# Two chunks of a linear-attention kernel: k and r turned by DMA transposes and not by TensorE

## The chip, the cores and the metric

The kernel runs on one core of a Trainium2 chip. The metric is device time in microseconds, the median of the runs; a profiled execution gives the span from its first to its last instruction and, beside it, that execution's own time.

## The reference, cut to what matters

A recurrent linear attention over 4 batches, 8 heads, 768 steps and 48 columns a head feeds a token and channel mixer. The inputs r, k, v are f32, the result is f32.

```
for t in range(S):
    cur = einsum('bhd,bhe->bhde', u[None] * kt, vt)
    y[:, :, t] = einsum('bhd,bhde->bhe', rt, state + cur)
    state = w[None, :, :, None] * state + einsum('bhd,bhe->bhde', kt, vt)
x = y.transpose(0, 2, 1, 3).reshape(B, S, H * D)
h = maximum(xt @ w_tok1, 0) @ w_tok2          # xt: x with steps and columns exchanged
u = x + h.transpose(0, 2, 1)
out = u + maximum(u @ w_ch1, 0) @ w_ch2
```

## The kernel before, in words

Each batch is cut into six chunks of 128 steps. A chunk's work: k, r and v are loaded (`kt`, `rt`, `vt`); k and r are multiplied by powers of the decay w into one bf16 tile `kr`; that tile is turned so that the head's columns lie on partitions (`rk`); TensorE multiplies the turned k and r to scores of step against step (`at_ps`); VectorE masks them (`AT`); TensorE multiplies `AT` and v, and the turned r and the carried state `S`, to `y_ps`; and the products of k and v are added to the state in `kv_ps`. The step's own term with u is formed beside it: `ku`, `rku`, a sum `adg`, and `yd`. The sum of `y_ps` and `yd` goes to `x_b`.

Then the mixer of the batch: `h_ps` and `h1r` (token mixing), `hx_ps` or `hT_ps` (back), a turned sum `uT`, `z_ps` and `zr` (up), `h_ps` and `osb` (down; these carry the name of the token tile in the profile), and a store. The mixer of one batch is interleaved with the chunks of the next: while TensorE does the second batch's mixer, GpSimd and the queues prepare the third batch's chunks, here called 0 to 5.

The third and the fourth batch take their chunks in pairs, (0, 1), (2, 3), (4, 5): one task writes the scores of both chunks of a pair. In these batches all products with k and r are made by GpSimd (POOL), in order.

How a chunk's `kr` is turned is told by the table `STYLES`, one entry a chunk. `pe` means eight transposes on TensorE into a PSUM bank `tr_ps`, followed by one copy to `rk` by VectorE or ScalarE. `dma` means one DMA transpose from `kr` to `rk`, issued by SyncE (SP). Before the change chunks 0 and 1 of the third batch are `pe`, and chunks 2 to 5 and the whole fourth batch are `dma`:

```
if STYLE[n][0] == "dma":
    L["rk"] = sb("rk", [128, 2, HP, T], bf16)
    sp.dma_start_transpose(L["rk"].rearrange("p j a s -> p (j a) s"),
                           L["kr"].rearrange("p j h d -> p (j h d)"))
else:
    for j in range(2):
        for a in range(HP):
            pe.transpose(L["tr"][:, j, a, :], pair(L["kr"][:, j], a), ident)
    copy(on, L["rk"], L["tr"])
```

All work is recorded as tasks first and then emitted in the order of the table `ORDER`, written out by hand; every engine runs its own instructions in that order, and waits by semaphores for the others. SP issues in one queue, in order, all loads of k, r and v, the DMA transposes of `kr` and of the mixer's `u_sb`, and the stores. `BUFS` gives each new tile its buffer: `m` are the seven PSUM banks that scores, `y_ps`, `z_ps`, `h_ps`, `hx_ps` and `tr_ps` share. `ENGINES` says who takes a task that two engines could do. Nearly all instructions carry line L287 of the profile, that of a helper, so they are told apart by tile names.

Of the kernel before, what the change touches and what calls it, by code (L numbers as in the profile page):

```python
# [11 lines left out]
f32 = mybir.dt.float32  # L12
# [6 lines left out]
Ln = ACTF.Ln  # L19

ORDER = [
# [41 lines left out]
]  # L63
BUFS = {
    'AT0': [
# [41 lines left out]
],  # L107
    'osb': [
    0, 1, 2, 2, 1, 0, 2, 1, 2, 0, 1, 2, 0, 2, 0, 1, 0, 1, 2, 1, 0, 2, 1, 0, 2,
# [32 lines left out]
    0, 1, 2, 1, 0, 2,  # L142
],
    'yd': [
    0, 1, 2, 0, 1, 2, 0, 1, 2, 1, 2, 0, 1, 2, 0, 1, 2, 0,
],
    'ydb': [
    0, 1, 0, 1, 0, 1,
# [15 lines left out]
]  # L164
W_DEP = [(0, 2, 2), (0, 5, 0), (0, 5, 0), (0, 3, 2), (1, 2, 0), (1, 1, 2), (1, 3, 0)]
HOLD = {(0, 4, 1): (0, 2, 1),
# [28 lines left out]
 [(0, 1), (2, 3), (4, 5)]]  # L195
STYLES = [
  ('f32', 'pe'), ('f32', 'pe'), ('f32', 'pe'), ('f32', 'pe'), ('f32', 'pe'), ('f32', 'pe'), ('f32', 'pe'),
  ('f32', 'pe'), ('f32', 'pe'), ('f32', 'pe'), ('f32', 'pe'), ('f32', 'pe'), ('pe', 'dve'), ('pe', 'dve'),
  ('dma', 'dve'), ('dma', 'dve'), ('dma', 'dve'), ('dma', 'dve'), ('dma', 'dve'), ('dma', 'dve'),
  ('dma', 'dve'), ('dma', 'dve'), ('dma', 'dve'), ('dma', 'dve'),  # L200
]
# [1038 lines left out]
```

## Time and profile before

| | |
|---|---|
| median of 3 runs | 163.56 us (163.2 to 163.7) |
| the profiled execution's own time | 162.75 us |
| its span | 161.0 us |
| TensorE busy, share of the span | 153.0 us, 95% |
| VectorE busy | 113.5 us, 70% |
| GpSimd busy | 89.3 us, 55% |
| ScalarE busy | 67.7 us, 42% |
| granted TensorE clock, mean | 0.997 |
| SP's and ACT's DMA queue, share of 16 engines | 70.3% |

The page cuts the span in 40 slices of 4.0 us. DMA landing is the time from the start of an issue to the last of its semaphore updates. SP has no busy time of its own: an issue is listed with its start and its duration, in which waits and a full queue are contained. A merged row, such as x2, reaches from the first start to the last end.

### The profile page before, as it was taken

The numbers are of one execution on the slowest core, as the hardware profiler recorded it, in microseconds if no ns is written. First come the engines' busy times: TensorE is split into PE (matmuls) and PEld (weight loads), VectorE is DVE, ScalarE is ACT, GpSimd is POOL, SyncE is SP. The second block draws the span as 40 slices with busy tenths as digits, with TensorE's granted clock in tenths as the row PEclk, the third lists the DMA queues.
The fourth block names the chain that finished last, engine by engine and source line by source line (L and its number), as shares of the span: only waits on it lengthen the run. The fifth ranks groups of instructions, "written<-read, shape, count | busy, mean of one in ns | idle before, by whom it ended". The sixth has DMA issues, their size and how long they took to land.

```text
span 161.0 us, 3815 instructions
## 1 busy us (share of the span) xinstructions
PE 153.0 (95%) x1475; PEld 102.1 (63%) x1475; DVE 113.5 (70%) x244; ACT 67.7 (42%) x150; POOL 89.3 (55%) x113
## 2 busy tenths in 40 slices
PE   6888789999999999999999999999999999999992
PEld 1354567776666777676776755766667666666661
DVE  6699695767574898789889876788988263852142
ACT  3977985567924243435144241047820202252000
POOL 7049892004788897999999998969422000000000
PEclk9999999999999999999999999999999999999998
DMA  4998899999999999999999997999620157200052
GB/s 124 202 213 165 149 206 211 210 209 196 224 210 211 173 232 178 252 236 171 186 193 224 196 184 150 240 201 197 137 77 4 49 122 219 98 4 0 0 195 98
DMA packets 90948, 26.35 MB, mean 164 GB/s; under 512 B 85682, under 2 KB 90036, under 8 KB 90932
## 3 DMA queue, kind: packets, MB, share of 16 engines
q1 hardware_dynamic: 88576, 22.88, 70.3%
q0 software_dynamic: 2160, 3.15, 11.7%
q8 instruction: 11, 0.18, 0.5%
q10 hardware_dynamic: 196, 0.11, 0.2%
q14 instruction: 5, 0.04, 0.1%
HBM read 20.46 MB, written 4.72 MB: 156 GB/s over the span
## 4 chain that ended last, share of the span: by engine, by line
PE 71%; DMA 10%; issue 9%; POOL 4%; ACT 2%; DVE 1%; SPq 1%; POOLq 0%
PE h_ps L287 34%; PE z_ps L287 23%; DMA vt<-in_v_dram 5%; DMA kt<-in_k_dram 5%; PE y_ps L287 4%; PE hT_ps L287 3%; PE at_ps L287 3%; PE kv_ps L287 2%; POOL wch L287 1%; POOL kr L287 1%; PE hx_ps L287 1%; PE tr_ps L287 1%; POOL pr L287 1%; PE trk L287 1%; ACT vb L287 1%
## 5 line engine op out<-in xcount | busy, mean ns | idle before, releaser
L287 PE MATMUL h_ps<-wch,zr 128*128 128x384 bf16 (+1 forms) x300 | 53.9, 320 | 0.0
L287 PE MATMUL z_ps<-uT,wch 128*128 128x384 bf16 x288 | 51.8, 326 | 0.0
L287 ACT ACTIVATE zr<-z_ps 128x384 bf16<-128x384 f32 x56 | 26.2, 492 | 41.8 <-PE z_ps L287 39.5
L287 PEld LDWEIGHTS <-wch 128*128 128x128 bf16 x288 | 31.4, 114 | 12.5
L287 PEld LDWEIGHTS <-zr 128*128 128x128 bf16 x300 | 27.4, 98 | 15.4 <-issue 0.2
L287 DVE TENSOR_TENSOR AT<-at_ps,mask 128x512 bf16<-128x512 f32 x48 | 30.6, 684 | 3.5 <-PE at_ps L287 2.9
L287 DVE TENSOR_SCALAR zr<-z_ps 128x384 bf16<-128x384 f32 x40 | 21.3, 553 | 12.5 <-PE z_ps L287 12.5
L287 POOL TENSOR_TENSOR kr<-kt,wnat 128x384 bf16<-128x384 f32 x20 | 19.9, 1005 | 2.8 <-DMA kt<-in_k_dram 2.7
L287 POOL TENSOR_TENSOR yd<-vb,adg 128x384 f32<-128x384 bf16 x17 | 13.9, 829 | 8.6 <-DVE x_b L287 4.2
L287 PEld LDWEIGHTS <-kr 128*128 128x128 bf16 x192 | 12.1, 97 | 6.8 <-DVE kr L287 1.8
L287 DVE TENSOR_TENSOR osb<-u_sb,h_ps 128x384 f32<-128x384 bf16 (+1 forms) x16 | 8.2, 526 | 9.7 <-PE h_ps L287 9.5
L287 ACT CAST vb<-vt 128x384 bf16<-128x384 f32 x22 | 11.0, 512 | 5.9 <-DMA vt<-in_v_dram 5.8
L287 POOL TENSOR_TENSOR rku<-ku,rt 128x384 f32<-128x384 f32 x12 | 12.0, 1000 | 0.2
L287 POOL TENSOR_TENSOR ku<-kt,u_bc 128x384 f32<-128x384 f32 x12 | 12.0, 1001 | 0.0
L287 POOL TENSOR_TENSOR kr<-rt,wp 128x384 bf16<-128x384 f32 x12 | 11.9, 1001 | 0.0
L287 DVE TENSOR_TENSOR x_b<-y_ps,yd 128x384 bf16<-128x384 f32 x18 | 9.5, 553 | 3.1 <-PE y_ps L287 1.4
L287 DVE TENSOR_TENSOR u_sb<-x_b,hT_ps 128x384 bf16<-128x384 bf16 x15 | 7.7, 551 | 4.5 <-PE hT_ps L287 4.4
L287 POOL DMA_DIRECT2D wch<-in_moe_w_ch_dram x5 | 3.4, 674 | 13.1 <-DMA kt<-in_k_dram 13.1
L287 PEld LDWEIGHTS <-wtok 128*128 128x128 bf16 x78 | 7.4, 98 | 4.5
L287 PE MATMUL h_ps<-x_b,wtok 128*128 128x384 bf16 x48 | 8.8, 326 | 0.0
L287 PE MATMUL y_ps<-vb,AT 128*128 128x48 bf16 x192 | 8.7, 183 | 0.0
L287 PEld LDWEIGHTS <-AT 128*128 128x128 bf16 x192 | 7.1, 96 | 0.3 <-DVE AT L287 0.2
(96 smaller groups left out, 180.4 us busy)
## 6 DMA issues: line engine op xcount, KB each, us to landing
kt<-in_k_dram SPq DMA_DIRECT2D x24, 192.0 KB, 4.2
vt<-in_v_dram SPq DMA_DIRECT2D x24, 192.0 KB, 4.0
out_dram<-osb SPq DMA_DIRECT2D x23, 192.0 KB, 2.2
win<-in_r_dram SPq DMA_DIRECT2D x6, 384.0 KB, 5.5
rt<-in_r_dram SPq DMA_DIRECT2D x12, 192.0 KB, 4.4
wch<-in_moe_w_ch_dram POOLq DMA_DIRECT2D x4, 384.0 KB, 6.1
wtok<-in_moe_w_tok_dram POOLq DMA_DIRECT2D x2, 384.0 KB, 6.8
wch<-in_moe_w_ch_dram POOLq DMA_DIRECT2D x1, 768.0 KB, 9.1
```

The source lines that it names most:

```text
L287: return lambda *args, **kw: tc.keep_in_program_order(f(*args, **kw))
```

## The change

The entries of chunks 0 and 1 of the third batch become `dma`. Two tasks fall away (the copies from PSUM), so later tasks get lower numbers, and the order and the buffers are written anew from there on.

```diff
 STYLES = [
...
-  ('f32', 'pe'), ('f32', 'pe'), ('f32', 'pe'), ('f32', 'pe'), ('f32', 'pe'), ('pe', 'dve'), ('pe', 'dve'),
+  ('f32', 'pe'), ('f32', 'pe'), ('f32', 'pe'), ('f32', 'pe'), ('f32', 'pe'), ('dma', 'dve'), ('dma', 'dve'),
...
 ORDER = [
...
-    306, 411, 414, 407, 412, 394, 307, 416, 532, 429, 536, 89, 330, 415, 92, 422, 533, 395, 417, 419, 431, 313, 88,
+    306, 411, 414, 407, 412, 394, 307, 416, 532, 429, 536, 330, 415, 89, 395, 417, 419, 533, 92, 422, 431, 313, 396,
...
```

The instructions of the first and the second batch, of the setup and of the fourth batch keep their order on every engine. What moves lies in the third batch's chunks and the second batch's mixer.

First, SP's queue from the middle of the second batch's last loads. `kr_72` is the tile of chunk 0, `kr_68` that of chunk 1, `kr_70` and `kr_71` those of chunks 3 and 2. Before:

```order
L287 DMA vt<-in_v_dram 128x8x48
L287 DMA rt<-in_r_dram 128x8x48
L287 DMA kt<-in_k_dram 128x8x48
L287 DMA out_dram<-osb 128x384 x2
L287 DMA rt<-in_r_dram 128x8x48 x2
L287 DMA_TRANSPOSE rk<-kr_70 128x8x128
L287 DMA_TRANSPOSE rk<-kr_71 128x8x128
L287 DMA kt<-in_k_dram 128x8x48
L287 DMA_TRANSPOSE uT<-u_sb 128x9x128
```

and now:

```order
L286 DMA_TRANSPOSE rk<-kr_72 128x8x128
L286 DMA vt<-in_v_dram 128x8x48
L286 DMA out_dram<-osb 128x384
L286 DMA rt<-in_r_dram 128x8x48
L286 DMA kt<-in_k_dram 128x8x48
L286 DMA_TRANSPOSE rk<-kr_68 128x8x128
L286 DMA rt<-in_r_dram 128x8x48 x2
L286 DMA_TRANSPOSE rk<-kr_70 128x8x128
L286 DMA_TRANSPOSE rk<-kr_71 128x8x128
L286 DMA_TRANSPOSE uT<-u_sb 128x9x128
```

Two transposes are new, one ahead of a `vt`, one ahead of the two `rt` of chunks 3 and 4; the two stores stand apart and earlier by a place or two; `uT` now stands ahead of the `kt` behind chunk 2's transpose. Six rows between the two `rt` and `kr_70` (vt, kt, out, rt, vt, kt), alike in both, are left out. All that follows, the transposes of chunks 4 and 5 with it, keeps its order.

Second, TensorE around the scores of chunks 0 and 1, matmuls alone. Before:

```order
L287 MATMUL tr_ps<-ident,kr_72 128x128
L287 MATMUL hx_ps<-ident,x_b_99 128x128
L287 MATMUL tr_ps<-ident,kr_68 128x128
L287 MATMUL hx_ps<-wtok_101,h1r 128x384
L287 MATMUL at_ps<-rk 128x128
L287 MATMUL hT_ps<-h1r,wtok_101 128x384
L287 MATMUL z_ps<-uT,wch_0_102 128x384
```

and now:

```order
L286 MATMUL hx_ps<-ident,x_b_99 128x128
L286 MATMUL hx_ps<-wtok_101,h1r 128x384
L286 MATMUL hT_ps<-h1r,wtok_101 128x384
L286 MATMUL z_ps<-uT,wch_0_102 128x384
L286 MATMUL z_ps<-uT,wch_1_103 128x384
L286 MATMUL at_ps<-rk 128x128
```

The two times eight transposes are gone, and the scores of chunks 0 and 1 now follow four `hT_ps` and nine `z_ps` matmuls (three z tiles) that stood behind them. The scores of chunks 2 and 3 move likewise, behind eight `h_ps` matmuls of the down projection and three small ones that stood behind them. Those of chunks 4 and 5 keep their place.

Third, VectorE from the last `x_b` of the second batch. Before:

```order
L287 TENSOR_TENSOR x_b_99<-y_ps,yd 128x384 x3
L287 COPY rk<-tr_ps 128x1024
L287 TENSOR_SCALAR h1r<-h_ps 128x384
L287 COPY osb<-h_ps 128x384
L287 TENSOR_REDUCE adg<-rku 128x8
L287 CAST uT<-hx_ps 128x3x128
L287 TENSOR_TENSOR AT_1445<-at_ps,mask 128x512
L287 TENSOR_TENSOR AT_1455<-at_ps,mask 128x512
L287 TENSOR_TENSOR u_sb<-x_b_99,hT_ps 128x384
```

and now:

```order
L286 TENSOR_TENSOR x_b_99<-y_ps,yd 128x384 x3
L286 TENSOR_SCALAR h1r<-h_ps 128x384
L286 COPY osb<-h_ps 128x384
L286 TENSOR_REDUCE adg<-rku 128x8
L286 CAST uT<-hx_ps 128x3x128
L286 TENSOR_TENSOR u_sb<-x_b_99,hT_ps 128x384
L286 TENSOR_SCALAR zr<-z_ps 128x384
L286 TENSOR_TENSOR AT_1443<-at_ps,mask 128x512
L286 TENSOR_TENSOR AT_1447<-at_ps,mask 128x512
```

The two copies from `tr_ps` are gone (the second stood behind `adg`), and the masks of chunk 0 stand behind one `u_sb` and one `zr`. On POOL only the product `kr_68` from `rt` moves, two places ahead; on ScalarE one store copy and one cast of v change places with their neighbours.

More of the change, by code (lines that the diff above doesn't have):

```diff
@@ L144 @@
     'yd': [
-    0, 1, 2, 0, 1, 2, 0, 1, 2, 1, 2, 0, 1, 2, 0, 1, 2, 0,
+    0, 1, 2, 0, 2, 1, 0, 1, 2, 1, 2, 0, 1, 2, 0, 1, 2, 0,
 ],
```

75 rows, old and new, of tables (BUFS, ENGINES, ORDER) are left out of this document.

## The prediction

> **What bounds the kernel now.** I read the slices of the page first, then the chain of waits, then what TensorE waits for, then SP's queue.
>
> ```profile
> span 161.0 us, 3815 instructions
> PE   6888789999999999999999999999999999999992
> DMA  4998899999999999999999997999620157200052
> ```
>
> TensorE is full from the seventh slice (24 us) to the last but one. The 16 DMA engines are full as well, up to slice 28 (113 us): two resources are at their limit at once. In the chain of waits, in order of time (start, us, what), all is TensorE from 43.98 on, but for 0.01 us of issue, until the last store:
>
> ```profile
> 43.98 0.40 PE trk L287 x4
> 63.37 0.45 PE tr_ps L287 x8
> 66.75 0.45 PE tr_ps L287 x8
> 68.51 0.55 PE at_ps L287 x16
> 69.49 0.49 PE z_ps L287 x3
> 78.65 0.55 PE at_ps L287 x16
> 87.08 0.55 PE at_ps L287 x16
> 92.19 3.90 PE h_ps L287 x24
> 157.83 0.02 issue
> ```
>
> The two `tr_ps` pieces are the transposes that go. The three `at_ps` pieces are the scores of the third batch's pairs (0, 1), (2, 3) and (4, 5). The `z_ps` piece is one tile of the up projection (0.49), and the `h_ps` piece gives 3.90 / 24 = 0.163 for a matmul of 384 columns. A microsecond taken from TensorE here, or put into its way, shows at the end. The windows 60 to 90 (engine busy with counts, then clock, DMA share, GB/s) and the one wait of TensorE after 44 us say the same:
>
> ```profile
> 60.00:70.00 10.00, 10.00 (x122) 7.09 (x121) 8.36 (x16) 3.98 (x10) 9.13 (x11) 1.00 1.03 216
> 70.00:80.00 10.00, 10.00 (x94) 7.00 (x93) 8.52 (x18) 4.03 (x9) 9.92 (x11) 1.00 0.99 193
> 80.00:90.00 10.00, 10.00 (x103) 6.86 (x100) 9.02 (x19) 3.42 (x8) 10.00 (x13) 1.00 1.20 212
> PE trk L287 <- DVE kr L287: 0.2, 1, 0.2
> ```
>
> In order: PE, weight loads, VectorE, ScalarE, POOL. TensorE is full, at a granted clock of 1.00; POOL has 0.95 us to spare in thirty; the DMA share is about 1 or more. So what is put on the DMA engines here has no idle time to go to, and all depends on how much lead the transfers have over TensorE.
>
> **What is removed.** Sixteen transposes leave TensorE: 0.45 + 0.45 = 0.90 us, on the chain. Their two copies leave VectorE, in the tile view of `rk`:
>
> ```profile
> L287 DVE COPY rk<-tr_ps x2: 679/680/682, 64.4 to 67.7; 128x1024 bf16<-128x1024 bf16 x2
> DMA to landing us min/median/max: 3.1/3.4/4.7
> ```
>
> That is 1.36 us off the chain, counted at nothing: TensorE is full through it. The second row is for the DMA transposes that the kernel has already.
>
> **What is added.** Two DMA transposes in SP's queue. Its issues (start, us, what) around the place, and later:
>
> ```profile
> 59.46 1.09 SPq L287 DMA_DIRECT2D vt<-in_v_dram  x1
> 60.60 1.72 SPq L287 DMA_DIRECT2D rt<-in_r_dram  x1
> 62.42 0.94 SPq L287 DMA_DIRECT2D kt<-in_k_dram  x1
> 63.41 1.19 SPq L287 DMA_DIRECT2D out_dram<-osb  x2
> 64.64 1.22 SPq L287 DMA_DIRECT2D rt<-in_r_dram  x2
> 69.11 1.00 SPq L287 DMA_DIRECT2D vt<-in_v_dram  x1
> 70.56 0.69 SPq L287 DMA_DIRECT2D kt<-in_k_dram  x1
> 71.36 4.01 SPq L287 DMA_TRANSPOSE rk<-kr  x2
> 75.43 0.57 SPq L287 DMA_DIRECT2D kt<-in_k_dram  x1
> 80.22 2.67 SPq L287 DMA_TRANSPOSE rk<-kr  x2
> 82.93 1.84 SPq L287 DMA_DIRECT2D rt<-in_r_dram  x2
> 91.58 3.69 SPq L287 DMA_TRANSPOSE rk<-kr  x2
> 95.32 0.57 SPq L287 DMA_DIRECT2D kt<-in_k_dram  x1
> 98.43 1.41 SPq L287 DMA_TRANSPOSE uT<-u_sb  x1
> ```
>
> Each issue begins as the one before ends; the only hole is 0.45 us, 70.11 to 70.56, until the queue waits for `u_sb` at 98.43. SP is thus always late here and waits for the transfers, not for engines. A transpose holds the queue from its start to the next start: (75.43 - 71.36) / 2 = 2.04 us, (82.93 - 80.22) / 2 = 1.36, (95.32 - 91.58) / 2 = 1.87. These are the bounds; the first pair also pays for the loads queued ahead of it, so I take the middle of the other two, 1.6 us. Two of them are 3.2; less the hole, everything behind them on SP is **2.75 us later** (2.27 to 3.63). Since SP waits for no engine there, nothing shortens this before 98 us.
>
> [...]
>
> **Who waits for what stands behind them.** Chunk 4's transpose is the second of the pair at 80.22; with a slot of 1.36 it is issued at 81.58. The transposes' landing times put it down at 85.0 (median) to 86.3 (longest). The load behind it:
>
> ```profile
> rt<-in_r_dram SPq DMA_DIRECT2D x1, 192.0 KB, 4.1
> ```
>
> is the one issued at 82.93, and lands at 87.0. A load's slot is (71.36 - 59.46) / 13 = 0.92 us, so I take 86.1 for the transpose before it. The scores that read it start at 87.08: a lead of **0.9 us** (0.7 to 2.1). After the change it lands at 86.1 + 2.75 = 88.85. TensorE would be there at 87.08 - 0.90 = 86.2, and has to wait. Behind these scores on TensorE stand down and up projections and all the rest; nothing else can run. The scores start 88.85 + 0.1 or so, and against before the end is 2.75 - 0.9 = **1.85 us later**; with the bounds, 2.27 - 2.1 = +0.2 to 3.63 - 0.7 = +2.9.
>
> The earlier pairs wait too, but these waits are parts of the same one, since SP's clock does not depend on TensorE. Chunk 1's transpose is issued after chunk 0's (59.46 + 1.6) and the slots of vt 1.14, rt 1.82, kt 0.99 and the two stores 1.23: at 66.2, landing 69.3 to 70.9. TensorE reaches its scores, moved behind four `hT_ps` (4 x 0.163 = 0.65) and three z tiles (3 x 0.49), at 68.51 - 0.90 + 2.12 = 69.7: a wait of nothing to 1.2, I take 0.3. Chunk 2's transpose is the second of the pair at 71.36 and lands about 77.3; now 80.0. Its scores, moved by eight `h_ps` matmuls (8 x 0.163 = 1.30) and three small ones (0.11), are reached at 78.65 - 0.90 + 1.41 = 79.2: a wait of 0.8.
>
> Moving these scores takes cover from the masks:
>
> ```profile
> 78.25 0.55 DVE L287 TENSOR_REDUCE adg<-rku 128x8 f32<-128x384 f32 x1
> 79.25 2.48 DVE L287 TENSOR_TENSOR AT<-at_ps,mask 128x512 bf16<-128x512 f32 x4
> 81.61 0.36 PE L287 MATMUL y_ps<-vb,AT 128*128 128x48 bf16 x8
> ```
>
> The four masks of a pair take 2.48 us, start 0.60 after the scores (78.65), and free the banks that `y_ps` and the next z tiles take. Between the scores and the last z tile that needs such a bank there will be 0.55 + 1.0 (kv, down) + 0.2 (y) + 2 x 0.49 = 2.7 us of TensorE work, and the masks are done after 0.60 + 2.48 = 3.08: a loss of 0.4 us even if every transfer were in time. It lies inside the wait at chunks 4 and 5 and costs nothing more; if that wait is not there, it comes off the gain of 0.90.
>
> **POOL.** The `rt` of chunk 3 is the first of the two issued at 64.64. It now stands behind both new transposes, 3.2 us later. POOL's rows:
>
> ```profile
> 62.91 1.00 POOL L287 TENSOR_TENSOR kr<-kt,wnat 128x384 bf16<-128x384 f32 x1 [0.39 <-DMA kt<-in_k_dram]
> 68.65 1.96 POOL L287 TENSOR_TENSOR kr<-rt,wp 128x384 bf16<-128x384 f32 x2
> 77.22 1.00 POOL L287 TENSOR_TENSOR rku<-ku,rt 128x384 f32<-128x384 f32 x1
> rt<-in_r_dram SPq DMA_DIRECT2D x4, 192.0 KB, 3.8
> ```
>
> The last is the landing of the four `rt` of 59 to 69 us: 64.64 + 3.8 = 68.4, now 71.6. POOL reaches the product at 68.65 - 0.39 = 68.3 (the wait for kt at 62.91 is filled by the moved product), so it waits 3.3 and is 3.0 us late from there. For the transposes that costs nothing: POOL's products are ready ahead of SP's later issue. But `rku`, ending at 78.2, ends at about 81.1, and the `adg` reduction stands ahead of the four masks on VectorE.
>
> **The sum.** -0.90 (transposes), +2.75 (queue), against the lead of 0.9 that the queue loses first and the 0.90 that TensorE has to wait as well: 2.75 - 0.9 = +1.85. On the profiled execution that is 161.0 to 162.9 of span and 162.75 to 164.6 of its own time; on the median, 0.8 us above that execution, 163.56 + 1.85 = **165.4 us**.
>
> **Rivals.**
> 1. *The DMA engines hide the transposes* (faster). If a transpose costs the queue less than the lead, the 0.90 remains, less the masks' 0.4: 163.56 - 0.5 = 163.1, at best 162.7. It decides from a shift under about 0.5 us, a quarter of a microsecond a transpose and the hole. For it: in SP's waits the first transpose at 71.36 is put down to 2.3 us of POOL, which would be idle time of the queue. Against: the `kr` it reads was done at 70.6 (68.65 + 1.96), and the DMA share is 0.99 to 1.20.
> 2. *A transpose costs no more than a load* (no change). Two slots of 0.92 less the hole are a shift of 1.4; with a lead in the middle of its bounds, 1.4, it is eaten up: 163.6. [...] For it: the lead may be 2.1. Against: three pairs of slots above 1.3.
> 3. *The wait sits on VectorE* (slower, other place). The queue's lead is large, but the `rt` of chunk 3 is late: `adg` ends at 81.6, the masks at 84.1, and the z tile that needs the last bank is followed by 0.49 + 0.37 + 1.95 + 0.17 + 0.65 + 0.49 = 4.1 us up to the scores of chunks 4 and 5: 88.2 and not 87.08, +1.1, 164.7. Against: it needs the same shift, and then the transpose is the later of the two.
>
> **How the numbers follow.** About 0.3%, 0.5 us, can be told from no change here. My forecast 0.57 (its own range 163.8 to 166.5), rival 1 0.13, rival 2 0.15, rival 3 0.15. Slower: nearly all of the forecast (0.55), 0.14 of rival 3, 0.03 of rival 2: 0.72. Same: 0.02 + 0.01 + 0.10 + 0.03 = 0.16. Faster: the rest of rivals 1 and 2, 0.12. The range for 8 in 10 starts at 163.0, inside rival 1, and ends at 166.6.
>
> **What would show it.** Right: in the profile after, TensorE has idle time before `at_ps`, ended by DMA `rk`, most of it before the scores at about 88 to 89 us; POOL waits some 3 us for `rt` near 68; SP's issues from 59 to 98 stay without holes, the pair for chunks 4 and 5 near 83. Wrong: TensorE without such waits, the pair's issue less than 1.5 us later than 80.22, or idle time before `z_ps` and `y_ps` that VectorE's masks end. A transpose slot under 1 us would refute the price; a wait at the fourth batch's scores would mean that the delay grows and my end is too early.

## The result, and the profile after

| | before | after |
|---|---|---|
| median of 4 runs | 163.63 us (163.2 to 163.75) | 165.40 us (164.53 to 165.82) |
| after / before | | 1.012, 95% interval 1.008 to 1.016 |
| profiled execution, own time (span) | 162.75 (161.0) | 164.53 (162.8) |

1.8 us slower by the medians, as forecast (165.4). Timed again beside later experiments, the ratio was 1.0143 (1.010 to 1.0187). What follows shows that the transposes in SP's queue are the cause, but that the number came out of terms that were not all right.

The page after, its first rows, and the three windows (PE, weight loads, VectorE, ScalarE, POOL busy, then clock, DMA share, GB/s):

```profile
span 162.8 us, 3785 instructions
PE   6888789999999999999899999999999999999992
DMA  4999899999999999998999999999750157200052
60.00:70.00 10.00, 10.00 (x106) 6.75 (x106) 7.23 (x14) 4.62 (x11) 8.28 (x9) 1.00 1.00 196
70.00:80.00 10.00, 9.80 (x86) 6.20 (x80) 7.42 (x14) 3.55 (x8) 8.79 (x10) 1.00 1.06 209
80.00:90.00 10.00, 9.00 (x100) 6.05 (x101) 8.45 (x18) 3.62 (x8) 10.00 (x12) 1.00 1.01 203
```

TensorE now has holes, 1.0 us of them between 80 and 90; POOL fell from 29.05 us in the thirty to 27.07. SP's transposes after (start, duration):

```profile
59.39 2.87 SPq L286 DMA_TRANSPOSE rk<-kr  x1
65.32 2.56 SPq L286 DMA_TRANSPOSE rk<-kr  x1
75.44 2.93 SPq L286 DMA_TRANSPOSE rk<-kr  x2
83.25 2.62 SPq L286 DMA_TRANSPOSE rk<-kr  x2
```

and, from the tile view of `rk`, their landing after the issue:

```profile
DMA to landing us min/median/max: 3.2/3.4/4.7
```

The pair of chunks 2 and 3 is issued 75.44 - 71.36 = 4.1 us later than before, that of chunks 4 and 5 83.25 - 80.22 = 3.0. The next rows say who waits, by engine (the bracket is the idle time before, and what ended it):

```profile
72.24 0.48 PE L286 MATMUL hT_ps<-h1r,wtok 128*128 128x384 bf16 x2
72.84 1.33 PE L286 MATMUL z_ps<-uT,wch 128*128 128x384 bf16 x7
80.49 0.62 PE L286 MATMUL at_ps<-rk 64*128 64x128 bf16 x16 [0.58 <-DMA rk<-kr]
85.02 2.37 PE L286 MATMUL z_ps<-uT,wch 128*128 128x384 bf16 x12 [0.27 <-DVE x_b L286]
88.63 0.56 PE L286 MATMUL at_ps<-rk 64*128 64x128 bf16 x14
71.13 1.95 POOL L286 TENSOR_TENSOR kr<-rt,wp 128x384 bf16<-128x384 f32 x2 [2.51 <-DMA rt<-in_r_dram]
80.74 0.55 DVE L286 TENSOR_REDUCE adg<-rku 128x8 f32<-128x384 f32 x1 [2.25 <-POOL rku L286]
81.21 2.47 DVE L286 TENSOR_TENSOR AT<-at_ps,mask 128x512 bf16<-128x512 f32 x4
84.41 0.56 DVE L286 TENSOR_TENSOR x_b<-y_ps,yd 128x384 bf16<-128x384 f32 x1 [0.26 <-POOL yd L286]
```

The only wait for a transpose is 0.58 us at the scores of chunks 2 and 3 (80.49). The scores of chunks 4 and 5 start at 88.63 with no wait. Behind 80.49 VectorE is the late one: masks from 81.21, the sum `x_b` at 84.41 behind a POOL that waited 2.51 us for r. Small losses hide inside "busy": two `hT_ps` matmuls take 2 x 0.163 = 0.33 us, but 0.60 pass from 72.24 to 72.84.

The chain of waits, all TensorE in this stretch before, now leaves it. Some of its pieces in order of time (start, us, what):

```profile
68.62 2.47 issue
71.13 1.95 POOL kr L286 x2
83.58 0.80 POOL yd L286
84.41 0.41 DVE x_b L286
86.25 1.14 PE z_ps L286 x6
```

The first piece, 2.47 us of issue, is POOL's wait for r. From 63.8 to 84.4 the chain runs through POOL, then through VectorE's sums to a z tile at 86.25; no transpose is on it.

### The profile page after: what moved, and what is told of

Read it like the earlier page. It is cut to its first block, busy times and chain, and to the rows that moved or that the text cites. A ratio compares the mean times of both kernels' runs of the same rounds, so it can differ in the third digit from the quotient of the medians.

```text
span 162.8 us, 3785 instructions
## 1 busy us (share of the span) xinstructions
PE 153.8 (94%) x1459; PEld 101.2 (62%) x1459; DVE 112.5 (69%) x242; ACT 68.2 (42%) x150; POOL 89.9 (55%) x113
## 3 DMA queue, kind: packets, MB, share of 16 engines
q0 software_dynamic: 2160, 3.15, 11.5%
## 4 chain that ended last, share of the span: by engine, by line
PE 52%; POOL 15%; DMA 13%; issue 12%; DVE 3%; ACT 2%; SPq 1%; POOLq 0%
PE h_ps L286 26%; PE z_ps L286 17%; DMA kt<-in_k_dram 8%; POOL kr L286 6%; DMA vt<-in_v_dram 5%; PE y_ps L286 2%; PE hT_ps L286 2%; POOL ku L286 2%; PE at_ps L286 2%; POOL rku L286 2%; POOL yd L286 1%; POOL wch L286 1%; DVE AT L286 1%; PE kv_ps L286 1%; DVE x_b L286 1%
## 5 line engine op out<-in xcount | busy, mean ns | idle before, releaser
L286 PE MATMUL z_ps<-uT,wch 128*128 128x384 bf16 x288 | 52.5, 326 | 0.7 <-DVE x_b L286 0.3
L286 PEld LDWEIGHTS <-kr 128*128 128x128 bf16 x176 | 11.1, 97 | 6.7 <-DVE kr L286 2.0
L286 DVE TENSOR_REDUCE adg<-rku 128x8 f32<-128x384 f32 x12 | 6.5, 548 | 3.8 <-POOL rku L286 3.7
```

Source lines behind the costliest of these rows:

```text
L286: return lambda *args, **kw: tc.keep_in_program_order(f(*args, **kw))
```

## The experiments

Each group was timed beside the kernel before on the same chip, and the groups on different chips; the median of the kernel before was 162.3 to 163.4, so the ratios are what compares. In us they are taken of 163.3.

| kernel | ratio to before (95%) | us |
|---|---|---|
| the change, first / again | 1.012 (1.008-1.016) / 1.0143 (1.010-1.0187) | +2.0 / +2.3 |
| order before, nothing turned | 0.9984 (0.9958-1.0011) | -0.3 |
| changed order, nothing turned | 1.0028 (0.9996-1.0061) | +0.5 |
| changed order, both transposes, three loads out | 1.0024 (0.9989-1.0059) | +0.4 |
| the change, r of chunk 3 first | 1.0092 (1.0057-1.0128) | +1.5 |
| transposes by DMA, scores not moved | 1.014 (1.0107-1.0173) | +2.3 |
| the same, SP's queue rewritten | 1.0215 (1.0162-1.0269) | +3.5 |
| chunk 0 alone by DMA | 1.0035 (0.9998-1.0072) | +0.6 |
| before, two more transposes | 1.0156 (1.0106-1.0207) | +2.5 |
| before, two more loads | 1.0062 (1.0035-1.0088) | +1.0 |
| the change / before, six stores on ScalarE's queue | 1.0084 (1.005-1.0117) / 1.0185 (1.0143-1.0228) | +1.4 / +3.0 |

**What TensorE's transposes are worth.** In the kernel before, for chunks 0 and 1:

```diff
-    L["tr"] = ps("tr_ps", ...); 8 x pe.transpose(L["tr"][:, j, a, :], ...); copy(on, L["rk"], L["tr"])
+    L["rk"] = wch2[:, 0:3, :] ... [:, 0:1024]      # a piece of the weights, nothing turned
```

> The kernel before with nothing turned for chunks 0 and 1: no transposes on TensorE, no copies, no DMA; their scores and outputs read a piece of the weights instead, so their numbers are meaningless. Order as before. What the change could gain at most: -0.90 us against before (ratio 0.9945), if all of TensorE's transposes lie on the chain. With the changed order the same omission gave +0.46; if the order's 1.1 to 1.4 us are real, the difference of the two shows them. Rival, that something else takes the place of the transposes at once: within 0.3 of before.

Measured 0.9984: 0.3 us at the middle, and no difference inside the interval; 0.9 us (ratio 0.9945) lies outside it. ScalarE's rows and TensorE's, then before's row for the same cast:

```profile
70.36 0.51 ACT L280 CAST vb<-vt 128x384 bf16<-128x384 f32 x1 [2.02 <-DMA vt<-in_v_dram]
70.78 0.48 ACT L280 ACTIVATE zr<-z_ps 128x384 bf16<-128x384 f32 x1
71.31 0.65 PE L280 MATMUL z_ps<-uT,wch 128*128 128x384 bf16 x3 [0.28 <-ACT zr L280]
```

```profile
70.07 0.51 ACT L287 CAST vb<-vt 128x384 bf16<-128x384 f32 x1 [1.05 <-DMA vt<-in_v_dram]
```

A TensorE that comes earlier makes ScalarE reach its cast of v earlier, but v comes no earlier: the wait grows from 1.05 to 2.02 us, `zr` stands behind it, and the next z tile waits for `zr`. The chain of before was all TensorE, and yet a load for another engine was just in time. That is one such wait seen in one profile; it accounts for 0.28 of the missing 0.6.

**What the moved scores cost.** The changed kernel with the two DMA transposes left out:

```diff
+    if n in (12, 13):
+        L["rk"] = wch2[:, 0:3, :] ... [:, 0:1024]; return
     L["rk"] = sb("rk", [128, 2, HP, T], bf16)
     sp.dma_start_transpose(...)
```

> The changed kernel with the two new DMA transposes left out: the scores and outputs of chunks 0 and 1 of the third batch read a piece of the weights in place of the turned k and r, so nothing has to be turned for them and these numbers are meaningless. All order on all engines as in the changed kernel. Queue theory: no wait for DMA at any score, GpSimd no longer late; TensorE saves 0.90 and loses 0.3 to 0.5 to the masks: 163.0 to 163.3 us. Rival, the moved scores cost the time by themselves: it stays at 164.5 to 165.4.

1.0028, 0.5 us, between the two forecasts. Against 0.9984 in before's order, the order takes 0.44%, 0.7 us at the middle; the two intervals just overlap, and the two were timed on different chips, so its size is uncertain. No DMA wait of TensorE is left. Its rows:

```profile
71.22 0.49 PE L286 MATMUL hT_ps<-h1r,wtok 128*128 128x384 bf16 x2
71.82 1.49 PE L286 MATMUL z_ps<-uT,wch 128*128 128x384 bf16 x8
80.38 0.36 PE L286 MATMUL y_ps<-vb,AT 128*128 128x48 bf16 x8
80.83 1.84 PE L286 MATMUL z_ps<-uT,wch 128*128 128x384 bf16 x9
71.09 0.68 DVE L286 TENSOR_TENSOR AT<-at_ps,mask 128x512 bf16<-128x512 f32 x1
79.49 2.48 DVE L286 TENSOR_TENSOR AT<-at_ps,mask 128x512 bf16<-128x512 f32 x4 [1.57 <-PE at_ps L286]
```

0.60 us for two `hT_ps` again, and 0.45 for eight `y_ps` that take 0.20 (81.77 to 81.97 in the chain of before). The z tile at 71.82 starts as the mask of 71.09 ends. VectorE idles 1.57 us until the scores come and is then 2.48 us at the masks, and the chain of waits runs through it from 79.49 to 84.16. So the late masks hold TensorE, as the prediction had it; the two gaps in these rows are 0.27 and 0.25 us, against its 0.4.

**Whether the cost is room in the queue.** The change with three loads behind chunk 0's transpose left out:

```diff
+    if (b, c, i) in ((2, 1, 2), (2, 4, 0), (2, 4, 1)):
+        loaded[b, c, i] = u_bc; return
```

> The changed kernel, both DMA transposes in place, with three loads left out that stand behind chunk 0's transpose in SP's queue: v of chunk 1, k and r of chunk 4 of the third batch; a constant tile is read in their place, so these chunks' numbers are meaningless. Three loads of 0.92 us take back the 2.8 to 3.0 us that the transposes cost the queue, 1.8 of it ahead of r of chunk 3. If the cost is the room that the transposes take in the queue and on the DMA engines: no wait of TensorE for the transposes of chunks 2 and 3, GpSimd's wait for r under 1 us; +0.2 to +0.7 us against before, as without the transposes. If a transpose costs by itself (its own late landing, what it does to others while it runs): +1.5 or more, as the change.

1.0024, the same as without the transposes (1.0028) within intervals of some 0.35% either way; TensorE waits for no transpose and GpSimd for no r. So with room made for them the two transposes cost nothing that can be measured. What they cost is the place of other transfers. One reservation: v of chunk 1, which stands right behind chunk 0's transpose and is one of the late transfers below, is itself left out here, so that not only room is made, and the three loads were not left out without the transposes.

**What a transpose and a load take there.** Before, with two more of the one or of the other at the change's two places:

```diff
+    sp.dma_start_transpose(t.rearrange("p j a s -> p (j a) s"), kr_of[2, 0].rearrange("p j h d -> p (j h d)"))
 or
+    sp.dma_start(h3(t), (k, r)[i][2, :, ts(i, T), :].rearrange("h s d -> s h d"))
```

> The kernel before, with nothing taken away, plus two DMA transposes of the same 256 KB each in SP's queue at the two places where the change puts them; their results are not used. TensorE keeps its transposes and the scores keep their places. Queue theory: SP is 3.0 us later from 70 us on, as in the changed kernel; chunk 2's transpose lands at 80.4 and not at 77.3, and TensorE, which reaches those scores at 78.6, waits 1.9; with the late products on GpSimd behind it up to 0.7 more: 165.5 to 166.2 us. Rival, the moved scores and late masks cost the time: 163.6. Rival, a transpose costs the queue no more than a load: 163.6.

> The same two places of the kernel before, but two more loads of 192 KB, results unused, in place of the two transposes. Queue theory with a load's slot of 0.92 us: two slots less the hole of 0.45 are 1.4 us; chunk 2's transpose lands at 78.7, TensorE is there at 78.6: 163.6 to 164.0 us. If only the number of issues in the queue counts and not their kind, it takes as long as the kernel with two more transposes.

1.0156 and 1.0062. SP's rows of the first, then of the second:

```profile
59.20 2.84 SPq L285 DMA_TRANSPOSE more<-kr  x1
75.80 2.69 SPq L285 DMA_TRANSPOSE rk<-kr  x2
```

```profile
58.85 2.42 SPq L285 DMA_DIRECT2D more<-in_k_dram  x1
74.07 3.17 SPq L285 DMA_TRANSPOSE rk<-kr  x2
```

From the first inserted issue to the pair of chunks 2 and 3 it is 16.60 and 15.22 us; before, the 13 issues alone take 71.36 - 59.46 = 11.90. A transpose thus costs the queue 2.35 us and a load 1.66. In the changed kernel it is (75.44 - 59.39 - 11.90) / 2 = 2.08. Neither price is a mean slot. It is not only the number of issues that counts: 2.5 us against 1.0, with intervals that don't meet. But a transpose moves 256 KB and a load 192, and by bytes the two prices are alike, 112 GB/s and 118; whether the kind counts beyond the size isn't shown.

The second kernel missed its forecast (0 to +0.4 us); the first met its number (+1.9 to +2.6), but not where it was expected: TensorE waits for no transpose there. In both a z tile waits behind `zr` and ScalarE's cast of a late v, for 2.0 us (the longest of the first) and 0.7. (The profiled execution with two more transposes took 167.12 us, far above its median of 164.87, so its waits and its price of 2.35 are uncertain.)

**Which waits carry it.** In the change, r of chunk 3 ahead of chunk 1's transpose:

```diff
-    rk<-kr (chunk 1), rt (chunk 3), rt (chunk 4)
+    rt (chunk 3), rk<-kr (chunk 1), rt (chunk 4)
```

> The changed kernel with one load moved: r of chunk 3 is issued ahead of chunk 1's DMA transpose and not behind it. GpSimd then waits about nothing in place of 2.5 us near 69 to 71 us; chunk 1's transpose lands 0.5 us later, and its scores wait that long, in place of the wait at the next scores. Theory that the late products of GpSimd cost 0.7 us of the loss (TensorE's waits near 85 and 86 us, behind the sums that wait for GpSimd): 164.7 us. Theory that SP's clock alone sets the end: 165.4.

POOL's wait for r falls from 2.51 to 0.43 us:

```profile
69.78 1.96 POOL L284 TENSOR_TENSOR kr<-rt,wp 128x384 bf16<-128x384 f32 x2 [0.43 <-DMA rt<-in_r_dram]
```

and the ratio to 1.0092, 0.3 to 0.5% under the change's two measurements, with intervals that overlap both. It points the way that was expected, at about the 0.7 us, and isn't proved. No wait of TensorE for a transpose is left, and 1.5 us of the loss remain: the chain of waits, without POOL in this stretch, now runs through VectorE's masks from 81.19 us on. The change, timed again:

> The changed kernel as it is, once more, beside the experiments of this group. +1.8 us against the kernel before (ratio 1.012), as measured first. The kernel without the two transposes but with the changed order came out at +0.46 us, the one with r of chunk 3 first at +1.5; both stand for parts of this difference if it is +1.8 here too.

Its profiled execution, 1.7 us longer in its span (164.5), shows a wait that the first one had not:

```profile
66.76 0.51 ACT L286 CAST vb<-vt 128x384 bf16<-128x384 f32 x1 [2.02 <-DMA vt<-in_v_dram]
67.30 0.49 ACT L286 ACTIVATE h1r<-h_ps 128x384 bf16<-128x384 f32 x1
67.84 0.34 PE L286 MATMUL hx_ps<-wtok,h1r 128*128 128x384 bf16 x1 [0.70 <-ACT h1r L286]
```

The v behind chunk 0's transpose is late, ScalarE's cast waits, and `h1r` behind the cast stops TensorE. So one delay of SP reaches TensorE by r (POOL), by v (ScalarE) and by the transposes, and how much it loses to each differs from one execution to the next (behind transposes 0.58 us in the first profile and 0.9 here, behind `h1r` none and 0.70). In both profiles of the change the chain of waits goes through POOL's wait for r (here from 70.37). Not all of it is SP's: here ScalarE's copy also waited 3.15 us for a store issued ahead of both new transposes (1.70 in the first profile), and TensorE lost 0.78 behind it.

**The scores back at their old place.** Before's order, the two transposes where the change has them:

```diff
-    pe.transpose x8 (chunk 0), pe.transpose x8 (chunk 1), two copies
+    sp.dma_start_transpose(chunk 0) ahead of vt (chunk 1);  sp.dma_start_transpose(chunk 1) ahead of rt (chunk 3)
```

> The kernel before with chunks 0 and 1 turned by DMA, the two transposes at the changed kernel's places in SP's queue, and nothing else moved but GpSimd's r product of chunk 1 (three places ahead): the scores and masks keep the places that they had before. Queue theory: chunk 1's transpose lands at 69.7, TensorE is at its scores at 67.5 and waits 2.2; it is then at the scores of chunks 2 and 3 at 79.9, and their transpose lands at 80.4; against before -0.9 + 2.2 + 0.5 = +1.8 us, and up to 0.7 more from GpSimd's lateness. Theory that moving the scores costs 1.1 us by itself and the queue the rest: the scores that are not moved save that, +0.7.

1.014, as the change: moving the scores neither helped nor hurt while the queue was late. The time is a little above the forecast (+1.8), but the wait of 2.2 us for chunk 1's transpose isn't there. It is 0.42:

```profile
70.17 0.60 PE L278 MATMUL at_ps<-rk 64*128 64x128 bf16 x8 [0.42 <-DMA rk<-kr]
```

with 0.39 just ahead of it behind a copy to `osb`, and 0.83 at `hx_ps` behind `h1r` and the cast of v, as above. A row of its windows, whose clock, 0.53, comes up below:

```profile
70.90:73.80 2.90, 2.90 (x11) 1.40 (x10) 1.16 (x3) 0.16 (x1) 2.04 (x3) 0.53 1.13 235
```

**A better order of the queue.** The same, with the urgent transfers first and three stores, two k and two r further back (T0 to T5 are the transposes of chunks 0 to 5, `out` a store):

```diff
-    kt, T0, vt, rt, kt, out, out, T1, rt, rt, vt, kt, out, rt, vt, kt, T3, T2, kt, uT, kt, vt, out, T5, T4
+    T0, kt, vt, rt, T1, rt, out, out, vt, kt, rt, kt, vt, T3, T2, out, kt, uT, rt, kt, vt, T5, T4, out
```

> As the kernel with the scores not moved, and SP's queue written anew so that what is needed first goes first: chunk 0's transpose one load earlier, chunk 1's right behind r of chunk 3 and ahead of r of chunk 2 and two stores; the transposes of chunks 2 and 3 ahead of a store, a k of the fourth batch and r of chunk 4; those of chunks 4 and 5 ahead of a store and another k of the fourth batch. Same transfers in all. Queue theory: what is late is only what stands behind the new transposes and is needed soon; chunk 1's lands at 68, a wait of 0.4; chunk 2's at 77.7, none; chunk 4's at 87, 0 to 0.9. -0.5 to +0.4 us against before, 1.4 to 2.3 better than the change. Rival, the full DMA engines make every transfer late whatever the order: +0.7 or more.

1.0215, the slowest of all by the middle; my list of what is urgent was wrong:

```profile
69.97 0.56 DVE L278 COPY osb<-h_ps 128x384 f32<-128x384 f32 x1 [4.55 <-DMA out_dram<-osb]
70.59 0.62 PE L278 MATMUL at_ps<-rk 64*128 64x128 bf16 x15 [2.06 <-DVE osb L278]
```

with a row of its windows, for later:

```profile
72.20:75.40 3.20, 3.20 (x12) 1.52 (x11) 2.07 (x4) 0.49 (x1) 3.02 (x4) 0.52 1.19 204
```

A store looks as if nobody waits for it. But it frees `osb`: with the two stores behind chunk 1's transpose, VectorE's next copy into it waited 4.55 us, the copy frees the bank that the scores need, and TensorE lost 2.06. The stores were urgent. (The change itself has them ahead of that transpose.) The rival isn't refuted: r and v were late here too, POOL waited 2.3 us for r, and `hx_ps` 0.92 behind the cast of v.

**Another queue for the stores.**

```diff
-STORE = ['SP', 'SP', 'SP', 'SP']
+STORE = ['ACT', 'SP', 'SP', 'SP']
```

> The changed kernel with the six stores of the first batch issued by ScalarE's queue and not by SP's; four of them stand between 57 and 72 us. Same transfers. If SP's one queue in order is what is short: SP is 2 to 3 us earlier at the transposes of chunks 2 and 3 (issue at 73 and not 75.4), +0.3 to +0.8 us against before. If the DMA engines' time is what is short, the shift stays and so does +1.8 to +2.3, with up to 0.5 more for ScalarE's issues.

> The same six stores on ScalarE's queue in the kernel before, for comparison: TensorE waits for no DMA there, so an earlier SP gains nothing; 0 to +0.5 us for the issues in ScalarE's way. If it is faster than before by 0.5 or more, the kernel before was held by SP's queue too.

1.0084 and 1.0185. SP's row in the changed kernel:

```profile
74.63 3.92 SPq L286 DMA_TRANSPOSE rk<-kr  x2
```

Issued at 74.63 and not near 73, the pair of chunks 2 and 3 isn't held by SP's own queue alone; but counted from chunk 0's transpose (60.06 here, 59.39 in the change) it comes 1.5 us earlier, and the ratio lies between both forecasts. TensorE's one wait of size, 1.7 us, is again at `hx_ps` behind the cast of chunk 1's v, which moved stores don't bring forward. For the kernel before neither theory had +1.85%. The kernel before with the stores moved, its issues over the whole run (queue, count, KB, us to landing) and one wait of ScalarE:

```profile
out_dram<-osb SPq DMA_DIRECT2D x17, 192.0 KB, 2.2
out_dram<-osb ACTq DMA_DIRECT2D x6, 192.0 KB, 4.1
```

```profile
64.72 0.48 ACT L287 COPY osb<-h_ps 128x384 f32<-128x384 f32 x1 [2.69 <-DMA out_dram<-osb]
```

The 2.2 us are no measure for the 4.1: most of the 17 stores left on SP run late. In the kernel before, 14 stores of 192 KB on SP are issued after 113 us, where the DMA row's digits are 0 to 7, and land after 2.0 us. Between 55 and 70 us, the four stores that the queue of ScalarE issues land after 4.0 us, and the four of the kernel before, on SP, after 3.4. ScalarE waits 2.69 us for its own stores, and TensorE 2.0 us behind it. Whether queue or engines limit stays open.

**Half of it.** Chunk 0 alone by DMA, in before's order, chunk 1 by TensorE:

```diff
+    if n == 12: sp.dma_start_transpose(...)      # at the change's place
```

> Half the change: the kernel before with chunk 0 alone turned by a DMA transpose, at the changed kernel's place in SP's queue; chunk 1 stays with TensorE and all else keeps its place. If the cost is the room in the queue, one transpose (1.5 to 2.9 us of SP, less the hole of 0.45) delays what stands behind it by 1.1 to 2.4 us; v and r loads are late by that for ScalarE and GpSimd, chunk 2's transpose lands at 78.4 to 79.7, TensorE is there at 78.15: +0.2 to +1.2 us against before. If the loads' lead takes up the first 1.5 us of it, and half of what leaving the transposes out altogether gave (0.26) remains: 0 to -0.2.

1.0035: about a quarter of the whole change's cost, inside the range of the queue theory, not faster. The stores again matter: VectorE's copy waits 2.57 us for `osb` at 68.9, and the scores of chunks 0 and 1 stop twice.

```profile
69.51 0.38 PE L278 MATMUL at_ps<-rk 64*128 64x128 bf16 x7 [0.66 <-DVE osb L278]
70.57 0.40 PE L278 MATMUL at_ps<-rk 64*128 64x128 bf16 x8 [0.68 <-DVE rk L278]
```

No variant that does the whole computation is faster than the kernel before. With TensorE's transposes worth 0.3 us there (0.7 at the end of the interval), little could be won.

## Why the prediction was right, and where it was not

The runs give a sum of their own, each term the difference of two kernels: -0.3 (nothing turned, order before), +0.7 (the order), +1.5 to +1.9 (the two transposes in the queue: 1.012 and 1.0143 less 1.0028). It ends at the measured +2.0 to +2.3 because the terms telescope; what is new is their sizes.

1. **The mechanism held in the large.** The two transposes hold SP's queue (2.08 us each), what stands behind them is issued late (4.1 and 3.0 us at the next two pairs), and TensorE pays (1.55 us at the scores of chunks 4 and 5). Without them, or with room made for them, most of the cost was gone (1.0028, 1.0024). The wait that carries the forecast's number, at the scores of chunks 4 and 5, was not there.
2. **The term -0.90 was mis-sized.** Sixteen transposes on TensorE's chain were worth 0.3 us. That a microsecond taken from TensorE shows at the end did not hold: what was just in time behind it then became the wait (v for ScalarE, 2.02 us, above). The forecast's total doesn't rest on this term, as an earlier TensorE was to wait that much longer; rival 1 does.
3. **The queue's shift of 2.75 us was too small at first.** 4.1 us at the pair of chunks 2 and 3, 3.0 at that of chunks 4 and 5. The slot of 1.6 was a choice near the middle; the first pair's 2.04, set aside because it "also pays for the loads queued ahead of it", came out right. The hole of 0.45 did not close: the changed queue has one of 0.49 (72.04 to 72.53). Two slots of 2.04 and no hole are 4.08. Nor did the shift last: the pair of chunks 2 and 3 held the queue for 4.07 us before (71.36 to 75.43) and for 3.02 after (75.44 to 78.46).
4. **The lead of 0.9 us was too small, and the place was wrong.** The step that has chunk 4's transpose landing at 88.85 and TensorE there at 86.2 failed on both sides. Issued at 84.6, it landed 3.4 us later, at 88.0; TensorE came at 88.63. The lead was read from the load behind the pair. The transposes issued between 70 and 98 us before have these landing times:

```profile
DMA to landing us min/median/max: 3.1/3.4/3.6
```

   This pair's own is not among them. By the median it lands at 85.0, and the lead is 2.1, an estimate; with the measured shift of 3.0 this wait would have cost 0.9 us and not 1.85.
5. **What made TensorE late was another path.** It reached these scores 1.55 us later than before (88.63 against 87.08), close to the 1.85 of a wait that did not happen: that is luck. Of waits that the profile names there are 0.58 at the scores of chunks 2 and 3 (0.8 was forecast) and 0.27 behind `x_b`; the rest is inside "busy". The chain runs by the late r, POOL, `yd`, `x_b` and a z tile. That is the way of the third rival, by sums and not by masks, and its sign, z tiles that VectorE holds up, is among those that the prediction gave for being wrong. POOL's wait was forecast at 3.3 us and is 2.51. The masks' 0.4 us were counted as hidden in the last wait; it did not exist, and the order's loss was on the chain. How the loss divides stays open: with r earlier, 1.5 of it remained.
6. **The rivals.** Hidden transposes: refuted, and the gain at stake was 0.3, not 0.9. A transpose as cheap as a load: refuted in price (2.35 against 1.66) and in time (1.0156 against 1.0062), with more bytes moved; and a load cost the queue 1.66 there and not 0.92. A transpose took 2.08 to 2.35 us of the queue for its 256 KB, 112 to 126 GB/s, in a queue that also carries loads and stores.

So the direction and the cause were right, and the time was right in part by luck: the shift was a little larger than forecast and the lead more than twice as large, so that the wait that was priced vanished, while late r and v and the moved masks cost about as much.

## What to carry to other kernels

A chain that is all one engine did not price what was taken out of it (0.90 us counted, 0.3 measured): before counting a removal in full, look for transfers that land just in time for any engine behind which the chain's buffers wait (v for ScalarE here, a wait of 1.05 us that grew to 2.02). With the DMA engines as full as here (a share of 0.99 to 1.20 from 60 to 90 us), the new transfers were paid by what stood behind them (+2.0 and +2.3 us, +0.4 with three of these loads out), so list every one of these with its lead, stores too: a copy waited 4.55 us for a buffer that a store frees. Price a new transfer by its bytes (112 GB/s for a transpose, 118 for a load) and by the most expensive slot near its place, which came closest here (2.04 us, against 2.08 to 2.35 measured), and not by the mean (0.92 for a load that took 1.66). And when the chain leaves the place that a forecast named, a time that agrees proves little (1.85 us priced for a wait that was not there).

## What had not been expected of the hardware

In three profiles the granted clock stood at half for about 3 us after waits of TensorE: 0.52 (72.2 to 75.4) with SP's queue rewritten, after waits of 0.92 and 2.06 us, and 0.53 (70.9 to 73.8) with the scores not moved, after 0.83, 0.39 and 0.42 (rows above). With two more transposes on SP, a window after a wait of 2.0 us shows the same:

```profile
75.80:79.00 3.20, 3.20 (x12) 1.44 (x10) 3.20 (x7) 0.98 (x2) 3.20 (x4) 0.53 1.04 207
```

With the scores not moved, the three matmuls of a z tile took 1.17 us at 71.31, and 0.65 in the kernel before at 69.33; over the window that is, as an estimate by its clock, 2.90 x (1 - 0.53) = 1.4 us. Whether it shows in the time is open: with the scores not moved, the profiled execution at a mean clock of 0.990 took 165.77 us, and one at 1.000 took 165.81. The low clock did not follow every such wait: with the stores on ScalarE's queue in the kernel before, one of 2.0 us ended at 65.3, and the clock stayed at 1.00:

```profile
PE tr_ps L287 <- ACT osb L287: 2.0, 1, 2.0
```

```profile
65.30:67.00 1.70, 1.59 (x15) 1.08 (x15) 0.07 (x1) 0.59 (x3) 0.94 (x2) 1.00 0.99 226
67.00:69.50 2.50, 2.29 (x21) 1.47 (x19) 2.01 (x4) 1.62 (x4) 2.50 (x3) 1.00 1.17 316
```

What decides when the clock falls, no run here tests.
